# A state-space layer beside a feed-forward block: the response's first transform moved behind the next pair's run, tables and late tiles in other steps, the last chunk's weights loaded earlier

## The chip, the cores and the metric

The kernel runs on one core of a Trainium2 chip. A core has TensorE (PE, matrix multiplication, with weight loads shown apart as PEld), VectorE (DVE), ScalarE (ACT), GpSimd (POOL) and SyncE (SP), each with its own instruction queue, and 16 DMA engines that all queues share. Each engine works through its queue in order: an instruction that waits at the head holds up all behind it. The metric is the device time of one execution in microseconds (us).

## The reference

The layer normalizes x (2048 rows of 576) and adds three things: x itself, a long convolution of the normalized rows along the 2048 positions, and a feed-forward block.

```python
x = A_u
xn = _layernorm(x, axis=-1)
return x + _A_ref(xn, A_re, A_im, B_re, B_im, C_re, C_im, log_dt, Dskip) + _B_ref(xn, w1, w2)

# _A_ref: a response K per channel, from 128 complex states
logdA, dB = dt * A, dt * Bc
K = einsum("dn,dnl,dn->dl", Cc, exp(logdA[:, :, None] * l), dB).real
y = irfft(rfft(pad(u)) * rfft(pad(K)))[:L] + u * Dskip

# _B_ref
out = silu(x @ w1) @ w2        # 576 -> 4608 -> 576
```

## The kernel before, in words

**The main line** is the feed-forward block (`ffn`, from line 233). The 2048 rows are taken in two halves of 1024, a half in two blocks of 512. The 4608 hidden columns are nine chunks of 512. For each half, chunk and block, `up` (line 283) multiplies the block by four w1 tiles into a PSUM tile `ph`, ScalarE applies SiLU (`gf`), and the result is kept as a rounded part `gh` and a rest `gl`. `down` (line 303) multiplies these by w2 into PSUM tiles `po`, and VectorE adds each to the accumulator `acc` (line 320). All large products run on fp32r operands that are split into a high and a low part, three matmuls for one; so each weight that arrives (`w1r`, `w2r`) is split into `w1h`/`w1l` and `w2h`/`w2l` by ScalarE and VectorE (lines 251 and 271). `po` has three PSUM buffers, `ph` two, and a third pool `pss` of three buffers serves all else.

Eight steps make up a block (`u0 d0 d1 d2 d3 u1 u2 u3`): the `down` of this block is interleaved with the `up` of the next. The table `after` (line 371) says behind which step of which block a piece of the next chunk is loaded or split. `w1r` has one buffer and holds two of a chunk's four w1 tiles at a time, `w2r` has two buffers for four w2 tiles.

**The side line** (`side`, line 811) is everything else, woven into those steps: a generator yields a fraction of the whole, and `weave` runs its next piece when the main line has come that far. The pieces are, in order:

1. the first eight row tiles are loaded, normalized and transposed (`phase0`, line 198);
2. while the first half's chunks run, the late row tiles 8 to 15 are loaded in pairs (`xj`), normalized, transposed by VectorE (`tr`) and stored (`dxt`, `dxn`) for the second half; and `natural` (line 396) turns A, B, C and dt into tables, in four parts. Its third part runs an arctangent, which on ScalarE needs tables other than those of SiLU;
3. `kgen` (line 519) builds the response in 36 steps of 16 channels: VectorE and ScalarE make sine, cosine and magnitude tables, and for every pair of steps TensorE contracts over the states into `kp` (line 631, 128 small matmuls of 128x32 weights). ScalarE copies `kp` to `kt`, and the first transform `z` follows (line 646, 8 matmuls of 64x128 weights, each two records in the trace). ScalarE copies `z` to `stage`, and every fourth step `stage` is stored to `d1k`. Beside it `spread` transforms the normalized rows (`pu`);
4. `spectral` (line 667) goes through 32 blocks of frequencies: `front` loads a block of rows and of response (`ur`, `kr`), splits them, transforms (`pu`, `pk`), multiplies, and the result is transformed back (`pb`) and stored to `d2`;
5. `tail` loads `d2` again (`ys`), makes the last transform (`py`) and adds it to the output.

`marks` (line 813) holds the fractions at which 3, 4 and 5 begin; `tail_at` those of the tail's loads and adds.

What stands where in each engine's queue is decided by a scheduler that runs over the whole program when it is built. `tc.high_priority()` lets an instruction go first among those that are ready, and `behind(ins)` keeps it behind a named one on its engine. So a piece that is moved to another step can move others.

Of the kernel before, what the change touches and what calls it, by code (L numbers as in the profile page):

```python
# [17 lines left out]
P = 128  # L18
# [23 lines left out]
def kernel(  # L42
# [155 lines left out]
    def phase0(p0, js):  # L198
        j0 = js[0]
        if j0 < 8:  # L200
            xs = load_x(j0, accp, "acc", (nc.sync, nc.scalar) if j0 < 4 else (nc.sync,))
            acc.update(zip(js, xs))
        else:
            xs = load_x(j0, p0, "xj", (nc.sync,))
# [28 lines left out]
    def ffn():  # L233
# [129 lines left out]
        for i, blk in enumerate(blocks):  # L363
# [4 lines left out]
            if half == 0 and c == NCH - 1:  # L368
# [27 lines left out]
    def natural(nat):  # L396
# [51 lines left out]
        yield  # L448

        with behind(pins["gh"]):  # L450
            nc.scalar.activation(r, ex, AF.Abs_reciprocal_sqrt, bias=neg1)
        nc.scalar.activation(r, r, AF.Square)
        for i in range(0, 4 * D, D):

            c = slice(i, i + D)
            e = nat.tile([P, D], F32, tag="lrT", name="e")
            v.scalar_tensor_tensor(e, ex[:, c], 1.0, r[:, c], op0=ALU.subtract, op1=ALU.mult)
            v.scalar_tensor_tensor(r[:, c], e, 2.0, r[:, c], op0=ALU.add, op1=ALU.mult)
            v.scalar_tensor_tensor(ex[:, c], ex[:, c], 1.0, r[:, c], op0=ALU.add, op1=ALU.mult)
        nc.sync.dma_start(dexp, ex[:, :3 * D].rearrange("n (d k) -> n d k", k=3))  # L460
        pr, pi, t0, t1 = tl("pr"), tl("pi"), tl("t0"), tl("t1")
# [17 lines left out]
        v.tensor_mul(t1, t0, t0)  # L479
        v.tensor_scalar(t1, t1, 1.0, None, op0=ALU.add)  # L480
        yield

# [36 lines left out]
    def kgen():  # L519
        fT, phiT = kf["f"], kf["phi"]  # L520
        with tc.tile_pool(name="kg", bufs=1) as kg:
# [54 lines left out]

            stage = None
            tabs = []
            nxt = head(0)
            al = powers(0)  # L580
            for i in range(NCK):
# [58 lines left out]
                z = [pss.tile([P, 512], F32, tag="pss", name="z") for _ in range(2)]  # L640
                first = None
                for eg in range(4):
                    for h in (1, 0):
                        rows = slice(64 * h, 64 * h + 64)
                        with tc.high_priority(), behind(first):
                            mm = nc.tensor.matmul(z[h][:, eg * P:(eg + 1) * P], kt[rows, eg * P:(eg + 1) * P], f1[rows],  # L646
                                                  start=True, stop=True, tile_position=(64 * h, 0))
                        first = first or mm.ins
                r = (i - 1) % NRUN
                if r == 0:  # L650
                    stage = kg.tile([P, 64, NRUN * CH], F32, tag="stage", name="stage")
                sv = stage[:, :, r * CH:(r + 2) * CH].rearrange("p k (e h c) -> p h e k c", h=2, c=2)
                for h in range(2):
                    nc.scalar.copy(sv[:, h], z[h].rearrange("p (e k c) -> p e k c", e=4, c=2))
                if r == NRUN - 2:
                    d0 = (i // NRUN) * NRUN * CH
                    kv = d1k.rearrange("(k n) (g d) -> g n k d", n=64, g=2)
                    for gp_ in range(2):
                        nc.sync.dma_start(kv[gp_, :, :, d0:d0 + NRUN * CH], stage[gp_ * 64:(gp_ + 1) * 64])
                yield (i + 1) / NCK  # L660

        nc.gpsimd.dma_start(d1k.rearrange("(k n) d -> n k d", n=P)[0],
                            dskip.unsqueeze(0).broadcast_to([32, D]), accum_op=ALU.add)

    def spectral():
        def front(k):
            if k % 2 == 0:
# [24 lines left out]

        mats = []
        nxt = front(0)
        for k in range(32):
# [47 lines left out]

    def load_split(rows, tag):
        t = kl.tile([P, D], F32, tag=tag + "r", name=tag + "r")
        nc.sync.dma_start(t, rows)
        return split_of(t, tag)

# [33 lines left out]
    def gate_of(i):  # L782

        return (FT + i * 2 * FT + 1) / (2 * NCH * 2 * 2 * FT)

    def side():
        nonlocal s4, kl, yp, pa, tail_at
        marks = (0.13, 0.595, 0.822)
        tail_at = (0.895, 0.0045, 0.922, 0.005)
# [8 lines left out]
        with tc.tile_pool(name="kf", bufs=1) as kfp:  # L798
            for n in ("f", "phi"):
                kf[n] = kfp.tile([P, D], F32, name=n + "T")  # L800
            with tc.tile_pool(name="nat", bufs=1) as nat, tc.tile_pool(name="pb", bufs=1) as pb:
                nt = natural(nat)
                tiles = iter(range(8, NJ, 2))
                for at, tables in ((0.0, 1), (0.02, 0), (0.035, 0), (gate_of(1), 1), (0.06, 0), (gate_of(2), 1), (0.08, 0), (0.085, 1)):
                    yield at
                    if tables:
                        next(nt, None)
                    else:
# [112 lines left out]
```

## Time and profile before

| | |
|---|---|
| median of 3 runs | 1129.48 us (1127.53, 1129.48, 1130.53) |
| the profiled execution | 1131.96 us; its span 1130.2 us, granted clock 0.996 |
| TensorE busy | 1106.7 us, 98% |
| VectorE busy | 917.1 us, 81% |
| ScalarE busy | 708.7 us, 63% |
| DMA | 148.56 MB, mean 131 GB/s |
| first matmul | 9.03 us after the start |

The span is the time between the first and the last instruction of the profiled execution. A matmul's busy time is longer than its step, because matmuls overlap: 128x288 has a mean of 297 ns, but such matmuls start 0.13 us apart. So a high busy share says that TensorE seldom stood still, and what it could still save is read from its waits and from the distances between starts. In a list of waits each row has the engine, the waiting instruction, what it waited for, the total in us, the number of times and the longest. In a timeline a row has start, duration, engine, line, operation, tiles and shape, number, and in brackets the idle time before it with what ended it. Line numbers are those of the kernel before.

### The profile page before, as it was taken

Reading aid. Unit: us, or ns where it says so; the run is one execution under the profiler, and the core shown is the slowest. Engines: PE = TensorE matmul, PEld = TensorE weight load, DVE = VectorE, ACT = ScalarE, POOL = GpSimd, SP = SyncE. Lnnn points to the kernel's source line nnn. Section 1 sums busy time; section 2 is a strip of 40 time slices with the busy share of each in tenths; the row PEclk is TensorE's granted clock in tenths of the full one; section 3 lists DMA queues with packets and bytes.
Section 4 is the critical chain, followed back from the end, with each engine's and each line's share of the span. In section 5 each row is a group of like instructions: output and inputs, shape, how many; then the busy total and the mean of one; then the engine's idle time right before and its main releaser. Section 6 shows DMA issues by size and latency. Waiting matters only on the chain.

```text
span 1130.2 us, 22881 instructions
## 1 busy us (share of the span) xinstructions
PE 1106.7 (98%) x9144; PEld 998.7 (88%) x9144; DVE 917.1 (81%) x1545; ACT 708.7 (63%) x1229; POOL 78.5 (7%) x130
## 2 busy tenths in 40 slices
PE   6999899999999999999999999999999999999998
PEld 5988799898888989999889998999999999998776
DVE  6698899999999999999999936887778778774433
ACT  4665356767677676676766727787777787772211
POOL 1110100000000000010000000000000000000110
PEclk9999899999999999999999999999999999999999
DMA  9346531334242625254743345554445455336971
GB/s 272 116 121 173 150 86 57 82 107 106 93 105 70 145 65 116 83 124 153 205 152 88 88 86 170 168 164 130 144 142 168 128 169 149 110 104 168 251 189 56
DMA packets 174971, 148.56 MB, mean 131 GB/s; under 512 B 110944, under 2 KB 141680, under 8 KB 174736
## 3 DMA queue, kind: packets, MB, share of 16 engines
q1 hardware_dynamic: 164768, 112.07, 37.6%
q0 software_dynamic: 9712, 34.14, 9.4%
q8 instruction: 72, 1.18, 0.4%
q10 hardware_dynamic: 384, 0.89, 0.3%
q14 instruction: 35, 0.29, 0.1%
HBM read 102.53 MB, written 44.61 MB: 130 GB/s over the span
## 4 chain that ended last, share of the span: by engine, by line
PE 86%; DVE 5%; DMA 5%; SPq 1%; issue 1%; ACT 0%; POOL 0%; DVEq 0%; POOLq 0%; ACTq 0%
PE po L316 36%; PE ph L291 30%; PE kp L631 3%; PE ph L292 3%; PE ph L293 2%; PE pk L754 2%; PE pu L754 2%; PE pb L754 2%; DMA w1r<-in_B_w_dram 2%; PE z L646 2%; PE pu L153 1%; DMA xj<-in_A_u_dram 1%; PE py L774 1%; PE pu L154 1%; DMA d1k<-stage 1%
## 5 line engine op out<-in xcount | busy, mean ns | idle before, releaser
L316 PE MATMUL po<-w2h,gh 128*128 128x288 f32 x1152 | 338.8, 297 | 6.4 <-DVE acc L320 5.7
L316 PE MATMUL po<-w2h,gl 128*128 128x288 f32 x1152 | 338.5, 297 | 1.0 <-DVE gl L301 1.0
L316 PE MATMUL po<-w2l,gh 128*128 128x288 f32 x1152 | 339.4, 296 | 0.0
L316 PEld LDWEIGHTS po<-w2h,gh 128*128 128x128 f32 x1152 | 216.1, 188 | 16.5 <-DVE acc L320 7.0
L316 PEld LDWEIGHTS po<-w2l,gh 128*128 128x128 f32 x1152 | 216.8, 188 | 4.3
L316 PEld LDWEIGHTS po<-w2h,gl 128*128 128x128 f32 x1152 | 216.5, 189 | 3.5 <-DVE gl L301 1.5
L299 ACT ACTIVATE gf<-ph 128x512 f32<-128x512 f32 (+1 forms) x148 | 86.5, 584 | 140.1 <-PE ph L293 124.7
L320 DVE TENSOR_TENSOR acc<-po,acc 128x288 f32<-128x288 f32 x288 | 126.3, 451 | 47.9 <-PE po L316 46.3
L291 PE MATMUL ph<-xh,w1h 128*128 128x512 f32 (+1 forms) x592 | 163.3, 391 | 0.5 <-ACT xh L123 0.5
L291 PE MATMUL ph<-xl,w1h 128*128 128x512 f32 (+1 forms) x592 | 161.5, 388 | 0.0
L291 PE MATMUL ph<-xh,w1l 128*128 128x512 f32 (+1 forms) x592 | 160.1, 386 | 0.0
L301 DVE TENSOR_TENSOR gl<-gf,gh 128x512 fp32r<-128x512 f32 (+1 forms) x148 | 98.7, 670 | 41.3 <-ACT gh L300 40.6
L291 PEld LDWEIGHTS ph<-xh,w1l 128*128 128x128 f32 x592 | 108.5, 189 | 20.1
L291 PEld LDWEIGHTS ph<-xl,w1h 128*128 128x128 f32 x592 | 108.5, 190 | 19.7
L291 PEld LDWEIGHTS ph<-xh,w1h 128*128 128x128 f32 x592 | 106.0, 191 | 20.0 <-issue 3.3
L300 ACT CAST gh<-gf 128x512 fp32r<-128x512 f32 (+1 forms) x148 | 89.5, 609 | 13.4 <-PE po L316 10.5
L278 ACT CAST w2h<-w2r 128x576 fp32r<-128x576 f32 x72 | 46.9, 672 | 30.6 <-PE po L316 19.5
L588 ACT ACTIVATE c<-th,magic 128x1040 f32<-128x1040 f32 x36 | 42.0, 1166 | 33.7 <-DVE C L611 25.7
L262 DVE TENSOR_TENSOR w1l<-w1r,w1h 128x640 fp32r<-128x640 f32 x72 | 56.9, 819 | 4.4 <-ACT w1h L260 4.3
L280 DVE TENSOR_TENSOR w2l<-w2r,w2h 128x576 fp32r<-128x576 f32 x72 | 53.4, 750 | 7.4 <-ACT w2h L278 7.2
L590 ACT ACTIVATE c<-th 128x1040 f32<-128x1040 f32 x36 | 38.7, 1076 | 32.6 <-DVE th L589 32.6
L292 PE MATMUL ph<-x,w1h 128*128 128x512 f32 (+1 forms) x148 | 57.2, 386 | 0.0
(182 smaller groups left out, 1836.9 us busy)
## 6 DMA issues: line engine op xcount, KB each, us to landing
w2r<-in_B_w_dram SPq DMA_DIRECT2D x72, 288.0 KB, 3.4
w1r<-in_B_w_dram SPq DMA_DIRECT2D x35, 512.0 KB, 3.9
d1u<-u POOLq DMA_DIRECT2D x32, 288.0 KB, 2.5
d1k<-stage SPq DMA_DIRECT2D x18, 512.0 KB, 7.7
ur<-d1u SPq DMA_DIRECT2D x32, 288.0 KB, 3.9
kr<-d1k SPq DMA_DIRECT2D x32, 288.0 KB, 2.8
d<-yo POOLq DMA_DIRECT2D x32, 288.0 KB, 3.9
ys<-d SPq DMA_DIRECT2D x32, 288.0 KB, 10.5
```

The costliest lines, as they stand in the source:

```text
L262: pins["w1l"] = nc.vector.tensor_sub(l1, src, h1).ins
L278: pins["w2h"] = nc.scalar.copy(h2, r2).ins
L280: nc.vector.tensor_sub(l2, r2, h2)
L291: nc.tensor.matmul(ph, w[:, kt, :], v[:, kt, a:e], start=n + kt == 0, stop=False)
L292: nc.tensor.matmul(ph, h1[:, 4, :], x4[:, a:e], start=False, stop=False)
L299: nc.scalar.activation(gf, ph, AF.Silu)
L300: pins["gh"] = nc.scalar.copy(gh, gf).ins
L301: pins["gl"] = nc.vector.tensor_sub(gl, gf, gh).ins
L316: pins["pe"] = nc.tensor.matmul(po[:, :HD], G[blk, t][g][:, js], W2[half, c, t][w][:, hs], start=n == 0, stop=n == 3 * FT - 1).ins
L320: nc.vector.tensor_add(acc[j][:, hs], po[:, :HD], acc[j][:, hs])
L588: nc.scalar.activation(c65, th, AF.Identity, bias=magic)
L754: nc.tensor.matmul(dst, st, mv[:, hs], start=n == 0, stop=n == 3 * len(terms) - 1)
```

## The change

Five places differ.

- `z` of a pair is no longer made right after its own `kt`: a function `transform` now makes it after the next pair's `kp`, with its matmuls in one chain behind the last of `kp`. `kt` gets a second buffer. The last pair's `z` comes after the loop.
- `natural` has five parts: the products of B and C and what follows from them (16 VectorE instructions, with two on ScalarE) become a part of their own, ahead of the part with the reciprocal root. The steps at which the parts run are new.
- A late tile has two pieces, its load and its normalization, which are placed singly; the first load comes at the beginning, and each further load in the step behind the normalization of the tile before.
- `spectral` begins with the loads of its first block; they are split 0.1 and used 0.12 of a unit later. `marks` go from 0.13, 0.595, 0.822 to 0.135, 0.6, 0.825.
- For the last chunk all six weight loads are issued in the first step, the second w1 half and the last two w2 tiles into buffers in the tail's pool.

```diff
-            r1 = (pa if first and t else wp).tile([P, 5, 2 * P], F32, tag="w1r", name="w1r", bufs=1)
+            last = half == 1 and c == NCH - 1
+            r1 = (pa if first and t else yp if last and t else wp).tile([P, 5, 2 * P], F32, tag="w1r", name="w1r", bufs=1)
...
-            r2 = (pa if first and t > 1 else wp).tile([P, D], F32, tag="w2r", name="w2r", bufs=2)
+            last = half == 1 and c == NCH - 1
+            r2 = (pa if first and t > 1 else yp if last and t > 1 else wp).tile([P, D], F32, tag="w2r", name="w2r", bufs=2)
...
+            if new == (1, NCH - 1):
+
+                after = {
+                    (0, "u0"): [(load_w1, 0), (load_w2, 0), (load_w2, 1), (load_w1, 2), (load_w2, 2), (load_w2, 3)],
+                    (0, "u1"): [(split_w1, 0)],
+                    (1, "u0"): [(split_w1, 2), (split_w2, 0)],
+                    (1, "d3"): [(split_w2, 1), (split_w2, 2)],
+                    (1, "u2"): [(split_w2, 3)],
+                }
...
+            def transform(kt, i, after):
+
+                nonlocal stage
+
+                z = [pss.tile([P, 512], F32, tag="pss", name="z") for _ in range(2)]
+                for eg in range(4):
+                    for h in (1, 0):
+                        rows = slice(64 * h, 64 * h + 64)
+                        with tc.high_priority(), behind(after):
+                            mm = nc.tensor.matmul(z[h][:, eg * P:(eg + 1) * P], kt[rows, eg * P:(eg + 1) * P], f1[rows],
+                                                  start=True, stop=True, tile_position=(64 * h, 0))
+                        after = mm.ins
...
-                kt = kg.tile([P, 512], F32, tag="kt", name="kt")
+                if kt is not None:
+                    transform(kt, i - 2, mm.ins)
+                kt = kg.tile([P, 512], F32, tag="kt", name="kt", bufs=2)
                 nc.scalar.copy(kt, kp)
...
                 yield (i + 1) / NCK
+            transform(kt, NCK - 1, None)
...
+        def operands(k):
+            rows = slice(k * P, (k + 1) * P)
+            return load_part(d1u[rows, :], "u"), load_part(d1k[rows, :], "k")
...
-            us, ks = load_split(d1u[k * P:(k + 1) * P, :], "u"), load_split(d1k[k * P:(k + 1) * P, :], "k")
+            us, ks = ops.pop(k) if k in ops else (split_of(t, n) for t, n in zip(operands(k), "uk"))
...
+        first = operands(0)
+        yield 1.1
+        with behind(pins["gh"]):
+            ops = {0: [split_of(t, n) for t, n in zip(first, "uk")]}
+        yield 1.12
         nxt = front(0)
...
-        marks = (0.13, 0.595, 0.822)
+        marks = (0.135, 0.6, 0.825)
...
-                tiles = iter(range(8, NJ, 2))
-                for at, tables in ((0.0, 1), (0.02, 0), (0.035, 0), (gate_of(1), 1), (0.06, 0), (gate_of(2), 1), (0.08, 0), (0.085, 1)):
+                def late(j):
+
+                    xs = load_x(j, pb, "xj", (nc.sync,))
+                    yield
+                    with behind(pins["gl"]):
+                        normed(pb, (j, j + 1), xs)
+                    yield
+
+                tiles = chain.from_iterable(late(j) for j in range(8, NJ, 2))
+                for at, todo in ((0.0, nt), (0.0, tiles), (0.004, tiles), (0.005, tiles), (gate_of(0), nt), (0.026, tiles), (0.028, tiles), (0.036, tiles), (0.038, tiles), (gate_of(1), nt), (0.06, tiles), (gate_of(2), nt), (0.09, nt)):
                     yield at
-                    if tables:
-                        next(nt, None)
-                    else:
-                        j = next(tiles)
-                        with behind(pins["gl"]):
-                            phase0(pb, (j, j + 1))
+                    with behind(pins["gl"] if at else None):
+                        next(todo, None)
```

More of the change, by code (lines that the diff above doesn't have):

```diff
@@ L1 @@
 import math
+from itertools import chain
 from contextlib import ExitStack, nullcontext
@@ L448, in natural @@
         yield
[L450 to L460, printed above, removed]
         pr, pi, t0, t1 = tl("pr"), tl("pi"), tl("t0"), tl("t1")
@@ L480, in natural @@
         v.tensor_scalar(t1, t1, 1.0, None, op0=ALU.add)
+        yield
+        with behind(pins["gh"]):
+            nc.scalar.activation(r, ex, AF.Abs_reciprocal_sqrt, bias=neg1)
+        nc.scalar.activation(r, r, AF.Square)
+        for i in range(0, 4 * D, D):
+            c = slice(i, i + D)
+            e = nat.tile([P, D], F32, tag="lrT", name="e")
+            v.scalar_tensor_tensor(e, ex[:, c], 1.0, r[:, c], op0=ALU.subtract, op1=ALU.mult)
+            v.scalar_tensor_tensor(r[:, c], e, 2.0, r[:, c], op0=ALU.add, op1=ALU.mult)
+            v.scalar_tensor_tensor(ex[:, c], ex[:, c], 1.0, r[:, c], op0=ALU.add, op1=ALU.mult)
+        nc.sync.dma_start(dexp, ex[:, :3 * D].rearrange("n (d k) -> n d k", k=3))
         yield
@@ L575, in head @@
                 return th
-            stage = None
+            def transform(kt, i, after):
[8 more added lines that the diff above has]
+                        after = mm.ins
+                r = (i - 1) % NRUN
+                if r == 0:
+                    stage = kg.tile([P, 64, NRUN * CH], F32, tag="stage", name="stage")
+                sv = stage[:, :, r * CH:(r + 2) * CH].rearrange("p k (e h c) -> p h e k c", h=2, c=2)
+                for h in range(2):
+                    nc.scalar.copy(sv[:, h], z[h].rearrange("p (e k c) -> p e k c", e=4, c=2))
+                if r == NRUN - 2:
+                    d0 = (i // NRUN) * NRUN * CH
+                    kv = d1k.rearrange("(k n) (g d) -> g n k d", n=64, g=2)
+                    for gp_ in range(2):
+                        nc.sync.dma_start(kv[gp_, :, :, d0:d0 + NRUN * CH], stage[gp_ * 64:(gp_ + 1) * 64])
+            stage = kt = None
             tabs = []
@@ L693, in spectral @@
         mats = []
+        first = operands(0)
+        yield 1.1
+        with behind(pins["gh"]):
+            ops = {0: [split_of(t, n) for t, n in zip(first, "uk")]}
+        yield 1.12
         nxt = front(0)
```

32 lines of the change are left out of this document (5 added, 27 removed).

## The prediction

> **What bounds the kernel now.** The page's first two parts come first: TensorE (PE) is busy 98% of the span, VectorE (DVE) 81%. The slices show why the second number misleads: from the 7th to the 23rd slice VectorE stands at 8 or 9 tenths. That is the stretch in which the response is built, and there both engines are full.
>
> ```profile
> PE 1106.7 (98%) x9144; PEld 998.7 (88%) x9144; DVE 917.1 (81%) x1545; ACT 708.7 (63%) x1229; POOL 78.5 (7%) x130
> ...
> PE   6999899999999999999999999999999999999998
> ...
> DVE  6698899999999999999999936887778778774433
> ```
>
> The chain that ended last is 86% PE, so what the change is worth is TensorE time. The view of waits on TensorE lists all that it waits for in mid-run:
>
> ```profile
> PE pt L122 <- DVE xn L189: 9.0, 1, 9.0
> PE po L316 <- DVE acc L320: 5.7, 2, 3.7
> PE pk L754 <- ACT kh L740: 1.3, 1, 1.3
> PE po L316 <- DVE gl L301: 1.0, 2, 0.7
> ```
>
> The 9.0 is the start, which the change leaves alone. The timeline places the others. The longest comes while the last late tile is normalized; TensorE runs at half rate behind it:
>
> ```profile
> 119.84 0.29 PE L316 MATMUL po<-w2l,gh 128*128 128x288 f32 x1
> 123.81 0.40 PE L316 MATMUL po<-w2h,gh 128*128 128x288 f32 x1 [3.67 <-DVE acc L320]
> ...
> 125.81 0.61 PE L316 MATMUL po<-w2h,gl 128*128 128x288 f32 x1 [0.67 <-DVE gl L301]
> 126.22 0.44 PE L316 MATMUL po<-w2h,gh 128*128 128x288 f32 x1
> ```
>
> VectorE at that moment (its own timeline): it stands 1.10 us before a tile that has not landed, and the eviction that TensorE needs is behind the statistics and a table product.
>
> ```profile
> 120.78 1.54 DVE L180 BATCH_NORM_STATS2 st<-xj 128x6 f32<-128x288 f32 x4 [1.10 <-DMA xj<-in_A_u_dram]
> 122.24 1.15 DVE L516 TENSOR_TENSOR wt<-wt,ex 128x576 f32<-128x576 f32 x1
> 123.30 0.45 DVE L320 TENSOR_TENSOR acc<-po,acc 128x288 f32<-128x288 f32 x1
> ```
>
> The other two waits end with a load that ScalarE stood before: the response's first block for the spectral stage, and the last chunk's second half of w1.
>
> ```profile
> 686.64 0.67 ACT L740 CAST kh<-kr 128x576 fp32r<-128x576 f32 x1 [4.50 <-DMA kr<-d1k]
> ```
> ```profile
> 1055.51 0.73 ACT L260 CAST w1h<-w1r 128x640 fp32r<-128x640 f32 x1 [4.40 <-DMA w1r<-in_B_w_dram]
> ```
>
> Last, a cost that no wait shows: TensorE's timeline where it leaves one tile shape for another.
>
> ```profile
> 236.45 0.31 PE L631 MATMUL kp<-S 128*32 128x64 f32 x6
> 236.69 0.40 PE L316 MATMUL po<-w2l,gh 128*128 128x288 f32 x1
> 236.93 0.30 PE L316 MATMUL po<-w2h,gl 128*128 128x288 f32 x1
> ...
> 240.78 0.29 PE L316 MATMUL po<-w2l,gh 128*128 128x288 f32 x1
> 240.99 1.16 PE L646 MATMUL z<-f,kt 64*128 64x128 f32 x16
> 242.09 0.40 PE L153 MATMUL pu<-sp,s 128*128 128x288 f32 x1
> 242.32 0.30 PE L154 MATMUL pu<-sp,s 128*128 128x288 f32 x1
> ```
>
> Starts of `po` are 0.13 us apart. Into `z` it is 0.21, and from the first full-size matmul behind `kp` or `z` to the second 0.24.
>
> **The change, part by part.** No matmul, eviction or cast is added, so every term is a wait or a switch.
>
> *The transform (`z`).* There are 18 pairs; each makes two excursions to small tiles, `kp` and later `z`. In the changed program's order 17 `z` runs stand right behind the next pair's `kp`, so 17 times one way out and one way in go. Out of `kp`: 0.15 to the first `po`, then 0.11 lost on the second (0.24 for 0.13). Into `z`: 0.08 to 0.09 over the usual step. Together 0.35, less the new step from `kp` to `z`, which no row shows. Its bounds are 0.01 (the pace within `kp`, 2.0 us for 125) and 0.22 (the longest way into `z` from a `po`); nearest is `kp` to `po`, 0.15, since it too leaves the shape of `kp`. So 0.20 x 17 = 3.4 us; ends 2.2 and 5.8. In the Trainium skill, TensorEngine Tiling, Key Properties, changing the tiling mode drains the engine. By that rule the step from `kp` to `z` still drains, which speaks for 3.4 and against 5.8. The trace agrees for the switches that it has (0.21 and 0.24 for 0.13). A second `kt` buffer covers the longer wait of each `kt`; without it the next copy would wait for this `z`. `z` now starts without waiting for ScalarE's copy (0.57 us), which lay under the `po` between and was no cost.
>
> *Tables and late tiles.* The same VectorE work is put in other steps, and each tile's load (four issues of 0.42 to 0.47 us on SP) goes a step ahead of its statistics. Tile 8 is normalized some 20 us earlier, where VectorE idled. What goes: 3.67 and 0.67 of waiting, and half of 125.8 to 131.9, when the clock was at 0.5: 3.0 us. Sum 7.4. What is late next: VectorE. I counted its rows between evictions (L320) in both orders, each at its mean duration less the 0.08 by which neighbours overlap (three evictions take 1.17, not 1.35). From the 22nd to the 33rd the changed order has 41.0 us of work against 34.5. TensorE took 41.5 there, so 34.1 without the 7.4; VectorE would be 6.9 behind. Three PSUM buffers of 12 matmuls (1.6 each) hide 4.8, which leaves a wait of 2.1, so this part gives -5.3. Bounds: no wait, -7.4; no cover, and so long a wait that the clock halves again, 6.9 + 3.0 - 7.4 = +2.5. On SP the new loads wait for the previous tile's eight `dxt` stores (about 0.5 each), and w1's pieces queue behind them. These wait for VectorE's split of the same buffer anyway (0.06 us after it at 60.17), which covers up to one tile's issue, 1.9 us; without the cover each us comes back on TensorE.
>
> *Spectral stage.* The first operands are now loaded at its start, split 0.1 later and used 0.12 later; before, load, split and use came in one step. From the last `z` to the first `pk` the order holds 28.3 us of matmul steps, before 21.9 (steps of 0.13 for 288 columns, 0.23 for 512). The 6.4 more exceed the 1.3 waited: -1.3, with 0 as the other end if ScalarE reaches the cast before the block and holds its evictions up. The last transform is now issued after the loop, at the mark, but its kt copy keeps the place, so stage, store, skip add on POOL and load (23 us from `z` to landing) begin no later. The first steps are due at once and the last `pb` stands 4.1 us of steps later; the tail's loads wait for it. But the first `py`, which uses them, moves too: 11.0 us of steps lie between, 12.6 before. TensorE did not wait there; if that margin was used up, 1.6 at most, and I take 0.
>
> *Last chunk.* All six loads are issued in the first step, with second buffers in a pool that is free; w1's half stands behind two `ys` pairs where six stood. It was issued at 1041.4 and used at 1055.5; now some 8 us sooner: -2.0 (the second wait of the 5.7), other end 0. Five issues (2.2 us) delay the later `ys`. Their third is issued at 1031, lands 10.5 after, and is used at 1049.8: covered by 6 us.
>
> *The response's second half.* TensorE arrives sooner, while VectorE is 95% busy (94.8 and 94.6 of 100 us in 400:500 and 500:600). By the same count its backlog peaks at 17 us near the 146th eviction, against 14 before, where TensorE did not wait. The 3 more could come at two peaks (the 129th has 16): 0 to 6; I take +1.5, half of one, as four `ph` groups (3.2 each) lie in between.
>
> Sum: -3.4 - 5.3 - 1.3 - 2.0 + 1.5 = -10.5 us. The profiled execution took 1131.96 (span 1130.2 and 1.8 around it), so 1121.5 for such an execution. It is 2.5 over the median, 1129.48, within the runs' scatter; for the median 1119.0.
>
> **Rivals.** *The early wait comes back at the response's start.* For it: 41.0 against 34.1, and VectorE without idle time in most of the stretch that follows (97.9 of 100 us in 200:300). Against: in 126 to 145 it had 6.6 us of idle time before the response's first instruction, which the new order fills. With a wait of 3.7 or more the clock halves too: that part gives 0 to +2.5, the total -5.2 to -2.7, 1124 to 1127. In the Trainium skill, TensorE: Matmul & The Clock Gate, Why this matters for your kernels, a gap above about 3 us brings the half clock. By that rule my 2.1 us wait costs no more than itself; the trace agrees (3.67 idle: 0.5; 1.98 idle at 1056: 1.00).
>
> *VectorE's backlog stops TensorE in the second half (slower).* Place: evictions 109 to 153, about 440 to 610 us. From the 109th to the 121st the changed order has 56.0 us of VectorE work against 45.2, and TensorE took 47.9. If each peak becomes a wait like that at 119.8, each costs 7.4. The total is then -12.0 + 7.4 per wait: one 1125, two 1132, three 1140. It decides from two on. Against: before, a backlog of 14 cost nothing.
>
> *The transfers stay late.* If the spectral block and w1 land as late as before, 3.3 us are missing: 1122. Against: the order has both ahead. That the transform isn't moved at all is excluded by that order.
>
> **How the numbers follow.** Forecast 0.60, the early wait 0.13 (half of it faster by over 0.3%), the backlog 0.21 (one wait 0.06, two 0.05, three or more 0.10), the transfers 0.06. One measurement of this kernel tells 0.3% (3.4 us) from no change. Faster 0.60 + 0.06 + 0.06 + 0.06 = 0.78; same, from the early wait and two backlog waits, 0.07 + 0.05 = 0.12; slower, from three on, 0.10. Best of all bounds: -5.8 - 7.4 - 1.3 - 2.0 = -16.5, 1113; with the runs' scatter 1112. Upward the range takes in the early wait and one or nearly two backlog waits: 1131. About 0.15 lies above it. The forecast's own range is 1113 to 1124.
>
> **What would show it.** After: 17 `z` runs starting about 0.15 us behind `kp`; no wait near 120 over 3 us and no 0.5 clock in mid-run; no wait of `pk` on `kh`; none on `acc` near 1045; VectorE near 100% busy in the response with few short waits of `po` on it. I am wrong if `po` waits for `acc` several times between 140 and 610 us, or if the clock falls there.

## The result, and the profile after

Seven executions of the changed kernel had a median of 1137.54 us (1132.05 to 1139.63), as many of the kernel before 1129.48 (1127.53 to 1130.95). The ratio is 1.0066 [1.0047, 1.0084]: slower, where 1119.0 and faster were forecast. The profiled execution took 1135.81 us (span 1133.9). It lies 1.7 below the median of its kernel, and that of before (1131.96) 2.5 above its own, so the two traces differ by 3.9 where the medians differ by 8.1. The traces tell where time went; how much is taken from the medians.

The page after (busy times, granted clock by slice, chain that ended last):

```profile
PE 1108.0 (98%) x9144; PEld 1000.1 (88%) x9144; DVE 917.7 (81%) x1545; ACT 707.8 (62%) x1229; POOL 73.6 (6%) x130
...
PEclk9999999999999999998999999999999999999999
...
PE 70%; DVE 13%; DMA 7%; issue 6%; ACT 3%; SPq 0%; POOL 0%; DVEq 0%; POOLq 0%; ACTq 0%
```

The dip of the clock that stood in the fifth slice has gone and another stands in the 19th. The chain was 86% TensorE and is 70%. What TensorE waits for in the changed kernel (total, times, longest):

```profile
PE pt L123 <- DVE xn L190: 8.9, 1, 8.9
PE py L799 <- DMA ys<-d: 4.5, 4, 2.0
PE po L316 <- ACT w2h L278: 3.8, 3, 2.3
PE po L316 <- DVE gl L301: 2.0, 2, 1.4
PE ph L291 <- ACT xh L124: 0.7, 1, 0.7
PE pu L154 <- ACT kt L674: 0.7, 3, 0.2
...
PE po L316 <- DVE acc L320: 0.2, 1, 0.2
```

The 5.7 on `acc` and the 1.3 on `kh` have gone, as forecast. Two rows over 0.5 us are new, `ys` and `kt`. A third has grown: the same view of the kernel before has a row on `w2h`, too, which the prediction's list leaves out.

```profile
PE po L316 <- ACT w2h L278: 0.7, 1, 0.7
```

To set stages against each other I add, over all neighbouring matmuls of a trace, the distance between their starts less the usual distance of the kind (0.1325 us for 288 columns, 0.2275 for 512). That is TensorE's lost time; its difference to the trace of before, plus up to 0.5 at the two ends, is the difference of the spans.

| us against before's trace | start to 140 | response, 140 to 660 | spectral, 660 to 1020 | tail, from 1020 | steps at `kp` and `z` |
|---|---|---|---|---|---|
| after | -6.8 | +9.0 | -1.4 | +4.3 | -1.1 |

Set against this one trace of before, the first 140 us and the spectral stage gave what they were to give, and the response and the tail took back more. (Two more traces with the same order up to 1027 us, of experiments below, show that before's trace was itself slow in the first two places. Against them the start gives 4.3 and 5.2, and the spectral stage nothing.) The worst place in the response, in the timelines of VectorE, SyncE, ScalarE and TensorE:

```profile
500.25 1.23 DVE L644 TENSOR_TENSOR S<-th,C 128x1024 f32<-128x1024 f32 x1 [1.15 <-ACT th L625]
...
507.13 1.42 DVE L280 TENSOR_TENSOR w2l<-w2r,w2h 128x576 fp32r<-128x576 f32 x2
```
```profile
507.90 0.99 SPq L269 DMA_DIRECT2D w2r<-in_B_w_dram  x2
```
```profile
511.65 0.67 ACT L278 CAST w2h<-w2r 128x576 fp32r<-128x576 f32 x1 [0.71 <-DMA w2r<-in_B_w_dram]
```
```profile
509.75 0.29 PE L316 MATMUL po<-w2h,gl 128*128 128x288 f32 x1
512.38 0.85 PE L316 MATMUL po<-w2h,gh 128*128 128x288 f32 x2 [2.34 <-ACT w2h L278]
```

VectorE splits two `w2r` tiles late, back to back. Only then are the two buffers free; the next load goes out at 507.90 and lands 3.7 us later, the cast follows, and TensorE stands still for 2.34. VectorE had itself stood idle for 1.15 until 500.25, waiting for ScalarE, so it had no backlog then. The split is late because ScalarE casts the two tiles only at 503.73 and because a table (`th`), an `sp`, a `gl` and evictions stand ahead of it in VectorE's queue. Around the end of TensorE's wait the clock halves for 6.83 us, which costs another 3.4; the windows before it and with it (columns: span, busy us of PE, PEld, DVE, ACT, POOL, granted clock, DMA share, GB/s):

```profile
502.00:511.76 9.76, 8.04 (x170) 6.75 (x169) 9.70 (x16) 6.97 (x12) 1.60 (x3) 1.00 0.50 151
511.76:518.59 6.83, 6.21 (x24) 6.11 (x25) 6.58 (x10) 5.25 (x9) 0.58 (x1) 0.50 0.53 90
```

In the tail, TensorE's and SyncE's timelines, and SyncE's of before:

```profile
1042.16 0.69 PE L799 MATMUL py<-ys,s 64*32 64x288 f32 x8 [0.33 <-DMA ys<-d]
...
1050.95 0.84 PE L799 MATMUL py<-ys,s 64*32 64x288 f32 x16 [1.09 <-DMA ys<-d]
1057.17 0.84 PE L799 MATMUL py<-ys,s 64*32 64x288 f32 x16 [2.01 <-DMA ys<-d]
```
```profile
1032.27 1.29 SPq L786 DMA_DIRECT2D ys<-d  x2
1034.24 1.23 SPq L786 DMA_DIRECT2D ys<-d  x2
1035.52 0.61 SPq L246 DMA_DIRECT2D w1r<-in_B_w_dram  x1
...
1039.42 1.95 SPq L786 DMA_DIRECT2D ys<-d  x2
```
```profile
1028.50 1.28 SPq L761 DMA_DIRECT2D ys<-d  x2
...
1030.47 2.80 SPq L761 DMA_DIRECT2D ys<-d  x4
```

The first `ys` goes out at 1032.27 (before: 1028.50), and the third pair, behind the weights, at 1039.42. The first `py` is no later by as much: 7.5 us lie between first issue and first use, before 9.15. From the second pair on TensorE waits (0.33, 1.09, 2.01), and behind the 2.01 the clock halves again (1057.9, 3.41 us).

### The profile page after: what moved, and what is told of

The parts are those of the page before. It is cut to its first block, busy times and chain, and to the rows that moved or that the text cites. A ratio compares the mean times of both kernels' runs of the same rounds, so it can differ in the third digit from the quotient of the medians.

```text
span 1133.9 us, 22870 instructions
## 1 busy us (share of the span) xinstructions
PE 1108.0 (98%) x9144; PEld 1000.1 (88%) x9144; DVE 917.7 (81%) x1545; ACT 707.8 (62%) x1229; POOL 73.6 (6%) x130
## 4 chain that ended last, share of the span: by engine, by line
PE 70%; DVE 13%; DMA 7%; issue 6%; ACT 3%; SPq 0%; POOL 0%; DVEq 0%; POOLq 0%; ACTq 0%
PE po L316 30%; PE ph L291 26%; DMA ys<-d 3%; PE ph L292 2%; PE ph L293 2%; PE pu L779 2%; PE pk L779 2%; PE pb L779 2%; PE kp L665 2%; DMA w2r<-in_B_w_dram 2%; DMA w1r<-in_B_w_dram 1%; DVE th L582 1%; DVE acc L320 1%; DVE S L644 1%; DVE C L633 1%
## 5 line engine op out<-in xcount | busy, mean ns | idle before, releaser
L644 DVE TENSOR_TENSOR S<-th,C 128x1024 f32<-128x1024 f32 x36 | 44.0, 1222 | 16.3 <-ACT th L625 16.1
```

Source lines behind the costliest of these rows:

```text
L644: nc.vector.tensor_mul(ov3, t[:, :, 0:64].rearrange("n d (x y) -> n d x y", y=32), mv3)
```

## The experiments

All were timed against runs of the kernel before on the same chip. The theory with which they began: the change wins what was forecast, and loses it in two places, (a) in the response, since TensorE now comes earlier to a VectorE that has no time to spare, and (b) in the tail, since the spectral stage ends later. The rival: one of the moved pieces costs by itself, wherever VectorE stands. The numbers of all runs first; the columns of stages are those above.

| kernel | median us | ratio to before, 95% | to 140 | response | spectral | tail | `kp`, `z` |
|---|---|---|---|---|---|---|---|
| after | 1137.54 | 1.0066 [1.0047, 1.0084] | -6.8 | +9.0 | -1.4 | +4.3 | -1.1 |
| after again | 1135.58 | 1.0064 [1.0042, 1.0085] | -5.4 | +6.9 | -1.4 | +4.7 | -1.1 |
| after without early loads | 1136.44 | 1.0064 [1.0047, 1.0082] | -6.1 | +5.6 | -1.5 | +6.8 | -0.9 |
| before + early loads | 1129.51 | 1.0004 [0.9987, 1.0021] | -2.5 | 0.0 | -1.6 | +0.6 | 0.0 |
| before + moved `z` | 1132.32 | 1.0025 [1.0013, 1.0037] | -1.3 | +4.8 | -1.6 | -1.8 | -1.1 |
| before + tables and tiles | 1131.49 | 1.0020 [1.0004, 1.0036] | -6.3 | +7.8 | -1.0 | -0.6 | +0.3 |
| after, `z` back | 1133.67 | 1.0035 [1.0022, 1.0049] | -6.3 | +1.7 | -1.6 | +4.3 | -0.1 |
| after, mark 0.815 | 1129.44 | 1.0003 [0.9989, 1.0017] | -6.5 | +7.3 | -1.6 | -0.5 | -1.1 |
| after, three `w2r` | 1131.97 | 1.0017 [1.0002, 1.0032] | -7.2 | +5.0 | -1.5 | +4.9 | -0.4 |
| after, `z` back, three `w2r`, 0.815 | 1123.30 | 0.9950 [0.9931, 0.9969] | -6.7 | +1.9 | -1.7 | -2.2 | +0.3 |
| after, three `w2r`, 0.815 | 1126.63 | 0.9977 [0.9967, 0.9988] | -7.5 | +5.7 | -1.6 | -0.9 | -0.7 |
| after without the phase | 1140.46 | 1.0098 [1.0079, 1.0117] | -6.1 | +7.0 | -1.6 | +5.2 | +4.7 |
| after, `z` back, 0.815 | 1125.94 | 0.9982 [0.9965, 0.9998] | -6.4 | +1.5 | -1.7 | -0.6 | -0.1 |
| before, three `w2r` | 1125.37 | 0.9968 [0.9957, 0.9979] | -8.2 | +3.3 | +0.8 | -3.0 | 0.0 |
| before, mark 0.812 | 1130.46 | 1.0008 [0.9996, 1.0020] | -1.6 | 0.0 | -1.3 | -0.1 | 0.0 |
| `z` back, three `w2r`, 0.815, again | 1123.47 | 0.9952 [0.9938, 0.9966] | -6.5 | +1.3 | -1.7 | -2.2 | +0.3 |

Two cautions for the whole table. Most edits let the scheduler order the program anew, so an edit also moves what it doesn't name. Five kernels made from before leave the spectral operands as they were; four of them show -1.0 to -1.6 there all the same, and the fifth +0.8. And one execution of an order differs from the next. "Before + early loads" and "before, mark 0.812" have before's order up to 1027 us, and yet show -2.5 and -1.6 in the start and -1.6 and -1.3 in the spectral stage. "After", "after again", "after without early loads" and "after, mark 0.815" have one order up to 680 us, and lose 5.6 to 9.0 in the response. So a column is good to some 3 us, and I rely on what returns in several pairs. A difference between two kernels of the table is given as that of their ratios, times 1129 us; the ratios go by all runs, so they can stand a little apart from the medians.

**The same kernel again.** No edit.

> The changed kernel once more, unaltered. Two theories of its loss. Tail theory: py waits 4.5 us for ys and the clock halves once behind it (1.7 us lost), against 2.0 us saved, so about +4 us of the +8. Backlog theory: VectorE's lag in the response holds SP's queue, w2 is loaded late, and the 2.3 us wait of po near 510 with the half clock behind it costs about 5.7 us. If both are steady, this profile shows both places again; if the second is a matter of chance in each execution, its place or its size changes while the waits of py on ys stay within 1 us of 4.5. Ratio to before 1.004 to 1.009 in both.

The ratio is the same, and so are the places: a wait of 2.4 on `w2h` at 510.9 with the half clock at 513.7, one of 2.4 on `ys` at 1054.5 with the half clock at 1056.4. Only the lengths of the half clock changed places (3.41 and 6.83 us). What is to be explained stands in the order of the program, not in one execution.

**Without the last chunk's early loads.**

```diff
-            if new == (1, NCH - 1):
-                after = {
-                    (0, "u0"): [(load_w1, 0), (load_w2, 0), (load_w2, 1), (load_w1, 2), (load_w2, 2), (load_w2, 3)],
...
-                }
```

> The changed kernel with the last chunk's six loads back in the steps that they had before (and in the old buffers). Tail theory: the waits of py on ys fall from 4.5 to under 1 us, the wait of 2.0 on acc near 1056 comes back, net about -4 us against the changed kernel: ratio to before 1.002 to 1.004. Backlog theory alone: the tail was no cost, the loss stays at 1.006 or more and the wait of po on w2h near 510 is still there.

The time didn't change, and the tail is worse (+6.8). The waits on `ys` shrink to 0.5, and in their place the second half of w1, now behind five pairs of `ys`, comes so late that one wait takes 6.26 (timelines of ScalarE, which stood 8.69 before that load, and of TensorE; VectorE makes the eviction that TensorE needs behind the split of the same load):

```profile
1057.44 1.35 ACT L258 CAST w1h<-w1r 128x640 fp32r<-128x640 f32 x2 [8.69 <-DMA w1r<-in_B_w_dram]
```
```profile
1060.18 0.61 PE L314 MATMUL po<-w2h,gh 128*128 128x288 f32 x1 [6.26 <-DVE acc L318]
```

So without the early weights the tail is no better. Whichever of the two transfers stands second is late.

**The early loads alone, on the kernel before.** The same lines added to it.

> The kernel before with the last chunk's six loads in the first step and nothing else of the change. If the loads themselves push ys back: py waits for ys 3 to 5 us, ratio 1.002 to 1.005. If ys is late in the changed kernel only because the spectral stage ends 4 us of steps later there: no wait on ys over 1 us, the 2.0 us on acc gone, ratio 0.998.

No difference (1.0004). The wait on `acc` near 1056 goes; 1.2 on `ys` and 1.7 of half clock (1075.6, 3.41 us) come. This part was forecast at -2.0 and is worth nothing.

**The moved `z` alone, on the kernel before.** The last pair's transform stays in its step.

```diff
-                z = [pss.tile([P, 512], F32, tag="pss", name="z") for _ in range(2)]
...
+                if kt is not None:
+                    transform(kt, i - 2, mm.ins)
+                kt = kg.tile([P, 512], F32, tag="kt", name="kt", bufs=2)
+                nc.scalar.copy(kt, kp)
```

> The kernel before with the first transform behind the next pair's run and nothing else (the last pair's transform stays in its step). Switch theory: 17 steps from kp to z of 0.15 us, about 3 us saved, no new wait: ratio 0.997. Backlog theory: VectorE has no room in the response, the 3 us come back as waits of po between 140 and 660 us, and one over 3 us halves the clock: ratio 0.999 to 1.005.

Slower by 0.25%, though the steps themselves are as cheap as forecast. The new waits in the response are 2.3 on `w2h` in three (a fourth, 1.1 at 97, lies ahead of it) and 2.0 on `kt` in two.

**Tables and late tiles alone, on the kernel before.** The change's edits in `phase0`, `natural` and the loop of late tiles, the first mark at 0.135, the others as before.

> The kernel before with the new steps of tables and late tiles, and the response beginning at 0.135 for 0.13; transform, spectral stage and last chunk as before. Early theory: the 3.7 us wait near 120 and the half clock behind it go, about 6.9 us as in the changed kernel's first 140 us. If VectorE has room for it in the response: ratio 0.994, no wait of po over 0.5 us between 140 and 660 us. If VectorE is the bound there: waits on w2h come as in the changed kernel (near 260 and 510) and the ratio is 0.998 to 1.002.

The first 140 us win 6.3, the response loses 7.8: the wins are paid back in full. The largest item is a wait of 3.7 on `w2h` at 574 with the half clock behind it.

**After with `z` back.** Each pair's transform behind its own `kt` again.

> The changed kernel with each pair's transform back behind its own kp. If the transform's place makes the waits of the response (kp and both z fill the three PSUM buffers, and VectorE's work is bunched): waits on kt vanish and those on w2h fall below 1 us, about -5 us against the changed kernel in spite of 3 us of switches, ratio 1.001 to 1.003. If TensorE's earlier arrival makes them: waits on w2h stay at 2 us or more and the ratio rises to 1.007 or more.

The response's loss falls to 1.7, from 9.0 in after's trace and 5.6 to 7.3 in the three others with its order, while 1.0 of switches comes back; the ratio falls by 0.0031, 3.5 us. The tail keeps its +4.3.

**After with the spectral stage's end at 0.815.**

```diff
-        marks = (0.135, 0.6, 0.825)
+        marks = (0.135, 0.6, 0.815)
```

> The changed kernel with the spectral stage's end mark at 0.815 for 0.825, so that its last store comes some 8 us sooner. Late-spectrum theory of the tail: py's waits on ys fall from 4 us to under 1 and the half clock near 1057 goes, about -5 us, ratio 1.001 to 1.003. If the order of the loads on SP alone is the cause: waits on ys stay at 3 us or more and the ratio at 1.006.

The ratio falls by 0.0063, 7.1 us, to that of no change. SyncE's timeline: the first `ys` goes out 5.9 us earlier, the third pair 5.1 earlier, and of the 4.5 on `ys` 1.7 are left.

```profile
1026.40 1.28 SPq L786 DMA_DIRECT2D ys<-d  x2
1028.37 1.23 SPq L786 DMA_DIRECT2D ys<-d  x2
...
1034.29 1.93 SPq L786 DMA_DIRECT2D ys<-d  x2
```

**After with three `w2r` buffers.** To make room, two constants (`halfpi`, `warm`) share a tile; this part of the edit is not printed.

```diff
-            r2 = (pa if first and t > 1 else yp if last and t > 1 else wp).tile([P, D], F32, tag="w2r", name="w2r", bufs=2)
+            r2 = (pa if first and t > 1 else yp if last and t > 1 else wp).tile([P, D], F32, tag="w2r", name="w2r", bufs=2 if last and t > 1 else 3)
```

> The changed kernel with three buffers for w2r in place of two (two constants share a tile to make room). Backlog theory: w2 is loaded late because its buffer comes free only when VectorE, behind in its queue, has split the tile before; a third buffer lets the load start before that: the waits on w2h (3.4 to 3.8 us) fall under 1 us and the half clock near 512 goes, -4 to -6 us, ratio 1.001 to 1.003. If the cast on ScalarE or another order makes the wait, the waits on w2h stay over 2 us.

The ratio falls by 0.0049, 5.5 us. The waits on `w2h` fall from 3.8 to 0.4, and no half clock is left in the response; but 2.3 on `kt` stand there instead of 0.7.

**All three together: `z` back, three `w2r`, mark 0.815.**

> After with three of its edits set otherwise: each pair's transform back behind its own kp, three w2r buffers instead of two, and the spectral stage ending at mark 0.815. Stages of TensorE's lost time against before were, in the traces so far: start to 140 us -6.3 and response +1.7 with the transform back, tail -0.5 with the earlier mark, spectral -1.6. If the loss in the response is the late w2r load behind a late VectorE, the parts add: response 0 to +2, no wait of po on w2h over 1 us, tail -1 to 0, total -6 to -9, ratio 0.992 to 0.995. Rival: whatever is won in the first 140 us is paid back in the response, because VectorE sets the pace of both together; then the response loses 5 to 8 by other waits (gl, x, acc) and the ratio is 0.998 to 1.002.

They add up in the main: 1123.30, faster than both kernels, and 13.1 below after by the ratios where the single edits gave 3.5, 5.5 and 7.1, so 16.1. What TensorE still waits for in mid-run:

```profile
PE ph L291 <- ACT gf L299: 1.7, 1, 1.7
PE po L316 <- ACT w2h L278: 0.9, 1, 0.9
PE ph L291 <- ACT xh L124: 0.7, 1, 0.7
PE po L316 <- DVE gl L301: 0.4, 1, 0.4
```

The rival (whatever the start wins the response pays back) falls with it: the start keeps 6.7, the response loses 1.9.

**Three `w2r` and mark 0.815, `z` left where the change puts it.**

> After with three w2r buffers and the spectral stage ending at mark 0.815, the transform left where the change puts it. The two edits alone gave -5.5 and -7 against after. If they mend two separate stalls, they add: 12 below after's 1137.5, so 1124 to 1127 and a ratio of 0.996 to 0.998; left over are the waits on kt and on VectorE that three buffers showed (response +5, tail 0, start -7). If the waits on w2h only moved elsewhere and the gain of three buffers was scatter, the ratio is 1.000 to 1.002, as with the mark alone.

1126.63, as two separate repairs would have it (by the medians; by the ratios 10.0 of the forecast 12). It differs from the kernel above in `z` alone, and shows what `z` costs: the response's +5.7, with 2.6 on `kt` in four waits. One of them, in ScalarE's and TensorE's timelines:

```profile
370.20 1.07 ACT L624 ACTIVATE c<-th 128x1040 f32<-128x1040 f32 x1 [1.50 <-DVE th L623]
371.30 1.07 ACT L625 ACTIVATE th<-th 128x1040 f32<-128x1040 f32 x1
372.28 1.15 ACT L626 ACTIVATE c<-c,hp 128x1040 f32<-128x1040 f32 x1
373.33 0.57 ACT L674 COPY kt<-kp 128x512 f32<-128x512 f32 x1
```
```profile
370.74 0.73 PE L596 MATMUL z<-f,kt 64*128 64x128 f32 x10
...
372.82 0.29 PE L316 MATMUL po<-w2l,gh 128*128 128x288 f32 x1
373.95 0.40 PE L154 MATMUL pu<-sp,s 128*128 128x288 f32 x1 [0.84 <-ACT kt L674]
```

`pss` has three PSUM buffers. `kp` and the two `z` behind it take all three in one stretch, so the next `pu` needs the buffer of `kp`, which is free when ScalarE has copied it to `kt`. That copy starts some 3 us after the last matmul of `kp`: it stands in ScalarE's queue behind three activations of 1.1 us, the first of which had waited 1.50 for VectorE.

**After without the phase.** The 36 additions of `phiT` to `th` (0.685 us each on VectorE) are left out.

```diff
-                with behind(pins["gl"]):
-                    nc.vector.tensor_add(split(th)[:, :, :, :32], split(th)[:, :, :, :32], col(phiT, i, 32))
```

> After without the addition of the phase to th (36 VectorE instructions of 0.685 us, 24.6 us of the 487 that VectorE works between 140 and 660 us); the output is another for that reason. If VectorE's backlog is behind the stalls of the response, the w2r buffers come free in time again, the waits on w2h (3.8 us in 3) go, and the half clock near 512 with them: response from +9 to between -3 and 0, total 9 to 12 below after, 1125 to 1128. If the stalls come from the moved transform itself (three PSUM buffers for kp and z, the load's own length), they stay with VectorE less busy: the waits on kt and w2h are there still and the total is within 3 us of after's 1137.5.

A miss. VectorE works 22 us less between 140 and 660; TensorE loses 2.0 less there, but 5.8 more at the switches, and the kernel is slower still (windows row 140:660, after and this one):

```profile
140.00:660.00 520.00, 515.18 (x5292) 465.25 (x5291) 487.43 (x732) 348.07 (x526) 21.54 (x39) 0.99 0.40 104
```
```profile
140.00:660.00 520.00, 513.91 (x5286) 462.55 (x5285) 465.55 (x693) 345.78 (x523) 23.60 (x42) 1.00 0.42 109
```

The waits on `w2h` fall to 1.1, which theory (a) asked for. But the scheduler's new order leaves `z` for a larger tile 26 times where after does so 19 times, and new waits come. The longest in the response, which the +4.7 at the switches includes, is again one for a PSUM buffer of `pss`, which ScalarE has to empty of a `pu` before `z` can have it:

```profile
432.22 0.76 PE L594 MATMUL z<-f,kt 64*128 64x128 f32 x2 [2.01 <-ACT u L156]
```

So a less busy VectorE is no cure by itself. The run doesn't tell how much of the response's loss VectorE's load is to blame for, since load and order changed together; that stays open.

**`z` back and mark 0.815, two `w2r`.**

> After with each pair's transform back behind its own kp and the spectral stage ending at mark 0.815; two w2r buffers as in after. It closes a square of four: with the transform moved, two buffers 1129.4 and three 1126.6; with it back, three buffers 1123.3. If the moved transform costs by itself (TensorE waits for the copy of kt because the three PSUM buffers go to kp and two z in one stretch) and the w2r buffer costs by itself, this one stands near 1123.3 + 2.8 = 1126. If the late w2r load comes about only with the moved transform (the response lost 1.7 with it back and two buffers), the third buffer is worth nothing here and it stands at 1122 to 1124.

The square is closed (median in us, ratio to before), the mark being at 0.815 in all four:

| | two `w2r` | three `w2r` |
|---|---|---|
| `z` moved | 1129.44, 1.0003 | 1126.63, 0.9977 |
| `z` back | 1125.94, 0.9982 | 1123.30, 0.9950 |

The moved `z` costs 2.4 with two buffers and 3.0 with three; the third buffer is worth 2.9 with `z` moved and 3.6 with it back. By the intervals each of these differences is good to 2 to 3 us. All four have the same sign, and there is no sign that either loss comes only with the other: they count as separate losses.

**Three `w2r` on the kernel before.**

> Before with three w2r buffers instead of two, nothing else. If two buffers are too few only because TensorE comes earlier to the response while VectorE is still full, there is nothing to win here: 1128 to 1131, ratio 0.998 to 1.002, response's loss still near 4.8. If three buffers are simply better for this kernel, and the fastest variant's gain is theirs and not the change's, it stands at 1123 to 1126.

The first expectation misses: three buffers win 3.6 here too, where TensorE waited only 0.7 on `w2h`. What goes is elsewhere: in this order the 3.67 on `acc` near 120 isn't there (start to 140: -8.2), nor the 1.98 on `acc` near 1056 (tail: -3.0), while the response loses 3.3. So the gain is not that of repairing the change. Whether the third buffer gives it or the new order that came with it (the order differs from 22 us on) isn't told.

**An earlier end of the spectral stage on the kernel before.**

```diff
-        marks = (0.13, 0.595, 0.822)
+        marks = (0.13, 0.595, 0.812)
```

> Before with the spectral stage ending at mark 0.812 instead of 0.822, nothing else: the mark that took 8.1, 7.7 and 5.3 us off three variants of after, moved as far on the kernel before. If those gains were the repair of the last pb that the change puts 4 us later, there is little to repair here: TensorE waited for no ys before, so 1127 to 1130, ratio 0.998 to 1.001, the tail's loss 3.5 to 5.5. If an earlier end is simply better for this kernel, it gains 5 or more here too: under 1124.

Nothing won, and nothing could be: the edit left the program as it was. The trace has the same instructions in the same order on every engine as that of before, and even the first `ys`, which goes out 2.8 earlier, keeps its place in the row (SyncE's timeline):

```profile
1025.66 1.28 SPq L761 DMA_DIRECT2D ys<-d  x2
...
1027.62 2.70 SPq L761 DMA_DIRECT2D ys<-d  x4
```

So this is the kernel before a second time, and what an earlier end would do to it stays untested. The 2.8 are what TensorE lost less in this execution, 1.6 in the start and 1.3 in the spectral stage: `pk` doesn't wait for `kh` here at all. The mark takes 7.1, 6.0 and 4.5 us off the three pairs of after's variants (two buffers, `z` back, three buffers), and the waits on `ys` fall with it from 4.5 to 1.7, 4.4 to 1.5 and 3.8 to 1.3. The kernel before waits for no `ys`, so it has no such wait to lose; that an earlier end isn't better for it in some other way is not shown.

**The fastest variant again.**

> The fastest variant again (transform back, three w2r buffers, mark 0.815), beside the kernel before on the same chip. Three buffers alone gave 0.9968 [0.9957, 0.9979]. If the rest of the change (tables and late tiles, early loads, spectral operands) is worth something of its own once its stalls are gone, this stays at 0.994 to 0.996, 1122 to 1124.5; if all of the gain is the third buffer's, it is at 0.996 to 0.998, 1125 to 1127.

0.9952 [0.9938, 0.9966]. Three buffers alone gave 0.9968 [0.9957, 0.9979]; the intervals overlap. The change's other parts are worth about 2 us in it, which is not firmly told apart from none.

So (b) holds in after's surroundings: in three pairs an earlier end of the spectral stage takes most of the tail's loss away. The rival holds for `z`, which costs wherever it was tried. Of (a) the chain by the `w2r` buffers is seen in the trace, and a third buffer takes its waits away; VectorE's own share in it stays open.

## Why the prediction was wrong

*The switches at `z`: right in size, wrong in what they cost.* The new step from `kp` to `z` takes 0.149 us in all 17 cases (0.15 was taken), and about 3 us go: 1.1 at the steps, and 17 x 0.107 = 1.8 on the second matmul behind, which the table counts in the response. But four pairs that differ in `z` alone say that the part as a whole costs: 2.8 us on the kernel before, 3.5 on after, 2.4 and 3.0 in the square. The step that failed is "A second `kt` buffer covers the longer wait of each `kt`". It looked at the SBUF tile. The PSUM tile that `kt` is copied from, one of three, was not counted, nor who needs it next. The 0.57 us copy that "was no cost" ahead of `z` became the thing that `pu` waits for. These waits are 2.0, 2.3 and 2.6 us in three kernels, but only 0.7 in after itself; there the waits on `w2h` fall from 3.8 to 1.7 when `z` goes back. How the rest of its 3.5 comes about is not shown.

*The response's second half: +1.5, 0 to 6.* The largest miss: +9.0 in the table, so 10.8 with the 1.8 that the switches gave there (7.4 to 9.1 by the three other traces with this order). Of the 10.8, 3.4 are waits on `w2h`, 3.4 the half clock behind the longest, 0.7 waits on `kt`; the rest is spread over shorter stalls. The term that failed is the wait itself: it was looked for on `acc` and sized by half a peak of the backlog, and it came on `w2h`, with half the clock behind it. The rival of VectorE's backlog had the place (509.8 lies in its 440 to 610 us), the kind of cost (a wait, then half the clock) and the sign, but watched `acc`: 0.2 us of waits. That its price for three waits, 1140, comes near the measured time is luck: there was one such wait, and the tail made up much of the rest. The delay was passed on through a buffer. VectorE's late split holds `w2r`, that holds back the load, and the load's own 3.7 us are added to the delay. Peaks of a backlog measured in evictions didn't show this, because the cover was counted in PSUM buffers, not in weight buffers. The list of waits that the prediction worked from might have pointed there, had it kept its row of 0.7 on `w2h`.

*The spectral stage: -1.3.* Right by luck: there is no wait on `kh`, and the stage gives 1.4 against the one trace of before that the prediction read. Neither of the two other traces with that order has the wait, and against them the stage gives 0.1 and -0.2. *The early wait: -5.3.* Right within its bounds: TensorE's lost time to 140 us falls by 6.8 against before's trace, by 5.2 and 4.3 against the two others, and in place of the 2.1 that was forecast there is a wait of 1.4 on `gl` at 121, with no half clock.

*The last `pb` 4.1 us later: 0, at most 1.6.* Wrong, and the largest item that an experiment puts a price on: the mark that undoes it takes 4.5 to 7.1 off three variants. The last `pb` itself was right (3.8 later, at 1028.59). The distance from the last `pb` to the first `py` was right (11.2 us measured, 11.0 worked out). The failed step is "Their third is issued at 1031, lands 10.5 after, and is used at 1049.8: covered by 6 us". The time of use came out (TensorE stood ready at 1049.86), but by luck: 1049.75 is the time in before's trace, and TensorE came no sooner only because the response had taken back what was won. The issue came at 1039.42. The loads' 2.2 us were put on the issue times of before, without the later `pb` that had been worked out a paragraph earlier (3.8), and between first and third pair the queue took 3.9 more, not 2.2. Two delays of one queue were priced one by one, each against the whole cover.

*The last chunk: -2.0.* The wait on `acc` goes, and one on `ys` takes its place; alone it is worth 0.

*The sum.* By the two traces, start, spectral stage and switches gave 6.8, 1.4 and 2.9: 11.1, against 10.0 forecast for them. Response and tail, forecast at +1.5 and -2.0, came to +10.8 and +4.3, 15.1 for -0.5: more than the whole of the traces' error of 14.5 (+4.0 for -10.5). By the means of all traces with the same order the three gave 4.8, 0.5 and 2.9, so 8.2, and the two came to +9.0 and +4.5. Response and tail are most of the error either way. The medians are 18.6 from the forecast (+8.1 for -10.5); what the traces don't show of that stays open. The runs scatter more than before (7.6 us from fastest to slowest, before 3.4).

## What to carry to other kernels

When a piece is moved next to another, list the buffers that both hold at that moment, PSUM included, and who asks for the next one: the wait moves to whoever comes third. Delays that meet in one DMA queue are added before they are set against the cover, and the cover is read at the last transfer of the row, not at the first. And where a scheduler orders the program, an edit's worth is only known from pairs with and without it in several surroundings; here a third buffer, with the order that came with it, was worth 3.6 us alone, and what was left of the five edits when their stalls were mended some 2 more. A wait in one trace is not yet a cost of the program: of the three traces with before's order, one had the 1.3 on `kh`. And before an edit's time is read, see in the trace that the edit changed the order at all.

## What the runs showed of the hardware

Half the clock came after shorter gaps than I had taken. Of the gaps of TensorE between 1.8 and 2.4 us in these traces, eight had a granted clock of 0.5 begin in them or within 3 us of their end (1.84, 2.01, 2.01, 2.14, 2.28, 2.34, 2.37, 2.39) and three had not (1.98, 2.05, 2.17); all six of 3.3 to 6.3 us had. Twice it came without a gap above 1.6 shortly ahead. Each time in mid-run it lasted 3.41 or 6.83 us, so 1.7 or 3.4 lost. Which of them is not set by the program: the wait near 510 us, in four traces with one order, was 2.34, 2.37 and 2.28 us with 6.83, 3.41 and 3.41 us of half clock, and 1.30 with none. The prediction took from the Trainium skill, TensorE: Matmul & The Clock Gate, Why this matters for your kernels, that a gap must exceed some 3 us, and from one gap of 1.98 that the trace agreed; measured here, a wait of 2 us must be priced at up to 5.4.
